# An attention and expert kernel whose order is made by a planner: a shared port in its rules, a shift per kind of task, and two pairs of heads in fp32

## The chip, the cores and the metric

The kernel runs on one core of a Trainium2 chip. The metric is the time of one execution in microseconds on the device; three executions of the kernel before are given by their median and their lowest and highest. The profile shows one further execution. Its engines are TensorE (PE, with its weight loads as PEld), VectorE (DVE), ScalarE (ACT), GpSimd (POOL) and SyncE (SP), which here issues nearly all transfers.

## The reference

Attention over 4 batches, 8 heads, 1152 keys and 64 dimensions, with queries averaged in pairs (576 of them), followed by a two-matrix expert layer with an ELU between:

```python
q_pool = q.reshape(B, H, S // 2, 2, D).mean(axis=3)
scores = np.matmul(q_pool, k.transpose(0, 1, 3, 2)) / np.sqrt(D)
attn = np.exp(scores - scores.max(-1, keepdims=True))
attn = attn / (attn.sum(-1, keepdims=True) + 1e-09)
x = np.matmul(attn, v)                      # (4, 8, 576, 64) -> 2304 tokens x 512
h = x @ w_in                                # 512 x 2048
g = np.where(h > 0, h, np.exp(np.minimum(h, 0)) - 1)
out = g @ w_out                             # 2048 x 512
```

All inputs and the output are fp32 (the weights arrive in a 64-bit form and are decoded on the chip).

## The kernel before

The work of a batch is cut into 4 pairs of heads, and a pair into 9 steps: 8 steps of 128 queries of one head (4 tiles, 2 heads) and one step with the last 64 queries of both heads. There are 144 steps in all. A step's tasks are: the scores on TensorE (L728 to L740), the score pass on VectorE (L746), which scales the scores from PSUM into the SBUF tile `ep` and keeps their extreme, the exponential with its sum on ScalarE (L752), and the reciprocal (L760, L761). Then one of two ways follows, by the table `SPLIT`, a letter for each pair of each batch:

- `s`, split: the probabilities are written as an fp16 high half `hb` (L791 on ScalarE or L788 on GpSimd) and an fp16 low half (L794, VectorE, a scale-and-subtract with two SBUF inputs); both are transposed by SP's DMAs (L800) into `pT`, and the product with the values takes 54 fp16 matmuls (L863). The values are split as well (L453, then L465 on VectorE or L411 with L471 on GpSimd).
- `f`, fp32: the probabilities are normalized in place (L764 GpSimd, L767 VectorE or L770 ScalarE), transposed on TensorE in 9 matmuls (L819), copied from PSUM into `pT` in three copies of 384 columns (L829 ScalarE, or a VectorE copy), and the product with the values is in fp32 (L851).

Keys, queries, expert inputs `x` and weights are always held as two fp16 halves, high and low, scaled by a power of two that a small chain finds (`across`: transpose, largest value, matmul back). The low halves of keys, queries and values run on VectorE (L465) or, as a scaling and a subtraction, on GpSimd (L411, L471). The expert layer of a batch is done in two groups of tokens (256 and 320), as soon as the attention outputs of all four pairs are there: first matrix (L965), ELU (L978, L981, L986, L991), high and low halves of `g` (L1005 or L1013; L1009 or L1017), second matrix (L1036), output.

The order of the work on every engine is not written out; a planner makes it. `Plan.add` records tasks with an engine, a duration, a key and, for some, other engines on which they may run. `Plan.run` then plays the program in time on five engines and at each moment gives a free engine the ready task of the lowest key; a task goes to another engine when that engine's duration plus a penalty is not over the work that stands ahead of it on its own. The order in which tasks start there is the order of the program. The numbers in `CFG` are offsets of the keys, penalties and step lengths. Durations of the class `Port` mark tasks that use the port that VectorE and GpSimd share. Before, two such tasks side by side were played at a reduced speed:

```python
def shares():
    d, p = busy["DVE"], busy["POOL"]
    if d is not None and p is not None and isinstance(d.dur, Port):
        return 0.72 if isinstance(p.dur, Port) else 0.55
    return 1.0
```

Of the kernel before, what the change touches and what calls it, by code (L numbers as in the profile page):

```python
# [19 lines left out]
    LOADS=-40491, WI0=-5900, WIT=9652, WO0=5372132, WOT=32390, T0=500, T1=500, M0=16259,  # L20
    M1=61275, KS=33293, KM=-17450, KE=21505, KH=-783, KL=19371, KV=-12117, KN=-1335, KX=-18428,
    KO=-16558, PEN=-19222, W0L=2523, WIN=5632, PD=20862, KS0=87938, KM0=-10021, KE0=9571,
    KH0=4598, KL0=8793, KV0=-437, KX0=-10633, PLM0=0, NS0=36, PLM=0, M2=5934, DP=0, FK=0,
    PENW=-13761, PENH=-11637, FL=2000, PH0=2, PH=1, KT=18640, KT0=8763, LV=45661, PENN=-27979,
    PENT=17079, PLP=1, WLP=1, HIP=0, PA=-1616, PB=6775, KA=-8245, KB=-28775, KC=3162,
# [3 lines left out]
SPLIT = ("ffff", "ssss", "ssss", "ssss")  # L29


class Port(float):
    pass
# [29 lines left out]
class Plan:  # L63
# [7 lines left out]
    def __init__(self):  # L71
        self.tasks, self.slots, self.make, self.lend = [], {}, {}, {}
# [43 lines left out]
    def run(self):  # L116
# [38 lines left out]
        while done < len(self.tasks):  # L155
# [5 lines left out]
            while again:  # L161
                again = False
                for e in engines:
# [29 lines left out]
                    rest[e] = float(t.dur)  # L193
# [15 lines left out]
            ends = [now + rest[e] / rate[e] for e in engines if busy[e] is not None]  # L209
# [13 lines left out]
            for e in engines:  # L223
# [3 lines left out]
                if rest[e] <= 1e-3:  # L227
                    t = busy[e]
                    busy[e] = None
# [22 lines left out]
def attention_moe_kernel(  # L252
# [165 lines left out]
    def across(src, n, key, after, bufs, take):  # L418
# [3 lines left out]
        def turn():  # L422
            nc.tensor.transpose(xp.ap[0:n, 0:128], src(), ident)

# [7 lines left out]
        t1 = plan.add("PE", 200.0, key, turn, after, [xp] + bufs)  # L432
        t2 = plan.add("DVE", 440.0, key, most, [t1], [xp, xr])
        t3 = plan.add("PE", 310.0, key, back, [t2], [xp, xr])
        return plan.add("DVE", 600.0, key, lambda: take(xp.ap[:, 256:256 + n]), [t3], [xp] + bufs)


    def prep(pr, t0, t1):
# [7 lines left out]
        def absum(dst, src, j):  # L446
            def f():
                nc.scalar.activation(out=dst(), in_=src(), func=AF.Abs, accum_out=sm.ap[:, j:j + 1])
            return f

        def hi(dst, src, j):
            def f():
                nc.scalar.activation(out=dst(), in_=src(), func=AF.Copy, scale=sm.ap[:, 8 + j:9 + j])  # L453

            def g():
                ts(nc.gpsimd, dst(), src(), sm.ap[:, 8 + j:9 + j], 1.0)
            return f, g

        def lo(dst, src, h, j):
            def f():  # L460
# [8 lines left out]
            def g():  # L469
                ts(nc.gpsimd, src(), src(), sm.ap[:, 8 + j:9 + j], 1.0)  # L470
                nc.gpsimd.tensor_tensor(out=dst(), in0=src(), in1=h(), op=ALU.subtract)  # L471
            return f, g

        def halves(n, kh, kl, dst_h, dst_l, src, j, after, bufs):
# [3 lines left out]
            t = plan.add("DVE", dve(n), kl, f, [h], bufs, [("POOL", Port(pol(n) + pol2(n)), g)] if CFG["PLP"] else [])  # L478
# [16 lines left out]
        def load(src, dst):  # L495
            def f():
# [3 lines left out]
            return f  # L500

        def qadd(eng):
            def f():
                qs = q32.ap[:, :nq, 0]
                eng.tensor_tensor(out=qs, in0=qs, in1=q32.ap[:, :nq, 1], op=ALU.add)
            return f
# [12 lines left out]
        sums.append(plan.add("ACT", act(1152) + 90.0, key[1], absum(k_h, k_s, 1), [tk], [kn, k32, sm]))  # L519
        if pr.split:  # L520
            v16 = pr.v16 = plan.buf("v16", "v32")
            v_s, v_h, v_l = (lambda: v32.ap), (lambda: v16.ap[:, :, :, 0]), (lambda: v16.ap[:, :, :, 1])
            sums.append(plan.add("ACT", act(1152) + 90.0, key[2], absum(k_h, v_s, 2), [tv, sums[1]], [kn, v32, sm]))
# [38 lines left out]
    for pr in pairs:  # L562
        if pr.i == 0:
# [4 lines left out]
    first_keys = pairs[0].kl  # L568

# [15 lines left out]
    def weights(which, g, t0, t1):  # L585
# [5 lines left out]
        for s in range(2):  # L591
            def load(s=s, raw=raws[s]):
# [7 lines left out]
            lds.append(plan.add("DMA", Move(490.0, 1700.0), CFG["W0L"] + s if g + which == 0 else t0 - 14000.0 + s, load, (), [raws[s]]))  # L600
# [285 lines left out]
    for st in steps:  # L886
        attention(st)
# [217 lines left out]
```

## Time and profile before

| what | value |
|---|---|
| median of 3 executions | 866.14 us (865.11 to 869.76) |
| the profiled execution | 859.8 us, span 857.9 us |
| granted TensorE clock, mean | 0.977 |
| busy TensorE / VectorE / ScalarE / GpSimd | 734.2 / 705.2 / 605.2 / 407.4 us |
| TensorE waiting for the score pass (L746) | 44.5 us in 45 waits |
| instructions | 19937 |

The profiled execution is some 0.7% shorter than the median of the others. Times of instructions are read from it, so a sum is made against 859.8 us and then put beside 866.1 us. A busy share counts the time in which an engine had an instruction running; that includes the time in which a running instruction stood still.

### The profile page before, as it was taken

The page shows a single profiled execution, that of the slowest core. Times are in us where ns is not written, and L with a number is a line of the kernel's source. Part 1 is how long each engine was busy: PE and PEld are TensorE (multiplying, and loading weights), DVE is VectorE, ACT ScalarE, POOL GpSimd, SP SyncE. Part 2 cuts the span into 40 slices and gives each one's busy share as a digit, 9 for nine tenths or more (in the row PEclk, how much of TensorE's full clock was granted, in tenths as well). Part 3 has the DMA queues.
Part 4 walks back from the last instruction along what each step waited for, and adds up shares of the span by engine and source line. Part 5 has one row for each costly group of instructions (what it writes and reads, how often), then busy time and mean ns, then how long its engine had stood idle before and what let it go on. Part 6 is the DMA issues. An engine that isn't in the chain of part 4 may idle for free. (4 is left out here: it accounts for less than half of the span.)

```text
span 857.9 us, 19937 instructions
## 1 busy us (share of the span) xinstructions
PE 734.2 (86%) x7839; PEld 474.3 (55%) x7839; DVE 705.2 (82%) x1308; ACT 605.2 (71%) x1019; POOL 407.4 (47%) x356
## 2 busy tenths in 40 slices
PE   1268789687978989997989999979998999999997
PEld 0136566466754565555765565547745655576553
DVE  7799898998998899988889698987998898975140
ACT  3478889898886788676788677777866775665250
POOL 1444343436999559313576364223764583035120
PEclk9999999999999999998999999979999999999999
DMA  8955719432959999998998999999889999950000
GB/s 284 264 111 154 194 34 295 157 76 36 218 129 168 179 176 225 177 192 180 183 178 168 200 181 210 191 187 219 170 162 169 216 153 158 185 106 2 25 2 31
DMA packets 353438, 136.06 MB, mean 159 GB/s; under 512 B 315200, under 2 KB 333632, under 8 KB 353344
## 3 DMA queue, kind: packets, MB, share of 16 engines
q1 hardware_dynamic: 353344, 134.79, 78.3%
q8 instruction: 61, 1.00, 0.5%
q14 instruction: 33, 0.27, 0.1%
HBM read 45.09 MB, written 4.72 MB: 58 GB/s over the span
## 5 line engine op out<-in xcount | busy, mean ns | idle before, releaser
L746 DVE TENSOR_SCALAR_CACHE_REDUCE ep<-s,sm 128x1152 f32<-128x1152 f32 x144 | 203.3, 1412 | 28.5 <-PE s L740 13.2
L752 ACT ACTIVATE ep<-ep,wk 128x1152 f32<-128x1152 f32 x144 | 180.4, 1253 | 51.5 <-DVE ep L746 42.7
L965 PE MATMUL r<-x,wi 128*128 128x256 f16 (+1 forms) x1536 | 203.6, 291 | 7.4 <-DVE x L876 2.3
L794 DVE SCALAR_TENSOR_TENSOR ep<-ep,wk,hb 128x1152 f16<-128x1152 f32 x108 | 174.3, 1617 | 14.6 <-POOL hb L788 8.0
L1036 PE MATMUL r<-wo,g 128*128 128x512 f16 (+1 forms) x888 | 179.7, 380 | 1.0 <-ACT x L872 1.0
L965 PEld LDWEIGHTS <-wi 128*128 128x128 f16 x1536 | 149.4, 99 | 53.5 <-issue 10.8
L728 PE MATMUL s<-kT,qT 128*128 128x512 f16 (+2 forms) x480 | 98.5, 338 | 50.0 <-DVE ep L746 44.5
L1036 PEld LDWEIGHTS <-g 128*128 128x128 f16 (+1 forms) x888 | 75.2, 100 | 89.9 <-issue 8.3
L791 ACT ACTIVATE hb<-ep,wk 128x1152 f16<-128x1152 f32 x68 | 85.1, 1252 | 51.6 <-issue 18.3
L788 POOL TENSOR_SCALAR hb<-ep,wk 128x1152 f16<-128x1152 f32 x40 | 56.4, 1410 | 123.8 <-DVE wk L761 66.1
L986 POOL TENSOR_SCALAR tmp<-tmp,us 128x320 f32<-128x320 f32 (+1 forms) x96 | 73.6, 769 | 84.5 <-ACT tmp L981 75.8
L863 PE MATMUL r<-pT,v 128*64 128x128 f16 (+1 forms) x3240 | 97.2, 218 | 3.7 <-DMA pT<-hb 3.2
L863 PEld LDWEIGHTS <-v 128*64 128x64 f16 x3240 | 87.9, 112 | 18.3 <-issue 17.4
L728 PEld LDWEIGHTS <-qT 128*128 128x128 f16 (+1 forms) x480 | 40.4, 101 | 92.6 <-issue 53.6
L991 DVE SCALAR_TENSOR_TENSOR tmp<-r,wk,tmp 128x320 f32<-128x320 f32 (+1 forms) x96 | 57.2, 607 | 32.4 <-POOL tmp L986 32.2
L978 ACT ACTIVATE tmp<-r 128x320 f32<-128x320 f32 (+1 forms) x96 | 45.6, 479 | 21.6 <-PE r L965 14.5
L819 PE MATMUL r<-ident,ep 128*128 128x128 f32 x324 | 48.4, 297 | 13.9 <-ACT ep L770 5.0
L981 ACT ACTIVATE tmp<-tmp,us 128x320 f32<-128x320 f32 (+1 forms) x96 | 58.2, 610 | 1.8
L740 PE MATMUL s<-kT,qT 64*128 64x512 f16 (+1 forms) x320 | 58.6, 404 | 0.0
L1017 DVE TENSOR_TENSOR g<-tmp,g 128x320 f16<-128x320 f32 (+1 forms) x49 | 43.3, 888 | 11.0 <-ACT g L1005 9.1
L819 PEld LDWEIGHTS r<-ident,ep 128*128 128x128 f32 x324 | 37.9, 150 | 23.9 <-issue 8.8
L829 ACT ACTIVATE pT<-r 128x384 f32<-128x384 f32 x108 | 45.9, 491 | 6.3 <-PE r L819 5.2
(125 smaller groups left out, 1017.8 us busy)
## 6 DMA issues: line engine op xcount, KB each, us to landing
k<-in_k_dram SPq DMA_DIRECT2D x16, 576.0 KB, 5.3
v<-in_v_dram SPq DMA_DIRECT2D x16, 576.0 KB, 5.4
q<-in_q_dram SPq DMA_DIRECT2D x32, 256.0 KB, 3.5
g<-in_moe_w_out_dram SPq DMA_DIRECT2D x14, 512.0 KB, 5.8
qT<-qT SPq DMA_DIRECT2D x48, 144.0 KB, 3.1
g<-in_moe_w_in_dram SPq DMA_DIRECT2D x13, 512.0 KB, 4.7
out_dram<-tmp SPq DMA_DIRECT2D x16, 256.0 KB, 2.7
pT<-hb SPq DMA_TRANSPOSE x108, 3.5
```

The lines of the kernel that those rows point to most:

```text
L728: nc.tensor.matmul(s.ap[rows, c, 0:n], pr.qT.ap[:, 0, j, rows], keys[h][c], start=True, stop=False, skip_group_check=True,)
L740: nc.tensor.matmul(s.ap[rows, c, 0:512], pr.qT.ap[r, 1, j, rows], keys[h][c][r], start=False, stop=True, skip_group_check=True,)
L746: nc.vector.tensor_scalar(e_(), s.ap.rearrange("p a b -> p (a b)")[:, 0:S], pr.sm.ap[:, 12:13], None, op0=ALU.mult, op1=ALU.min, accum_out ...
L752: nc.scalar.activation(out=e_(), in_=e_(), func=AF.Exp, bias=nm.ap[:, 0:1], scale=-1.0, accum_out=nm.ap[:, 1:2],)
L791: nc.scalar.activation(out=hb.ap, in_=e_(), func=AF.Copy, scale=nm.ap[:, 1:2])
L794: nc.vector.scalar_tensor_tensor(out=e16(), in0=e_(), scalar=nm.ap[:, 1:2], in1=hb.ap, op0=ALU.mult, op1=ALU.subtract)
L819: nc.tensor.transpose(tp.ap[:, c * 128:(c + 1) * 128], e_()[:, (j + c) * 128:(j + c + 1) * 128], ident)
L863: nc.tensor.matmul(half(h), pr.v16.ap[:, h, order[c], e], p, start=(j + c == 0), stop=(j == 2 and c == NCH - 1), skip_group_check=True,)
L965: nc.tensor.matmul(hp.ap[:, f * n:(f + 1) * n], w_in16[g][:, a, c, (f0 + f) * 128:(f0 + f + 1) * 128], x16.ap[:, e, c, g0:g0 + n], start=( ...
L981: nc.scalar.activation(out=en.ap[:, :m], in_=en.ap[:, :m], func=AF.Exp, scale=us.ap[:, 8 + g:9 + g])
L986: nc.gpsimd.tensor_scalar(en.ap[:, :m], en.ap[:, :m], -1.0, us.ap[:, 5:6], op0=ALU.add, op1=ALU.mult)
L1036: nc.tensor.matmul(op.ap[r0:r0 + tn, :], gt[qd].ap[:, a, fi, o:o + tn], w_out16(f // 2)[:, e, f % 2, :], start=(i < 128 // tn), stop=(i >= ...
```

## The change

The planner's model of the shared port becomes a turn: a VectorE task marked `Port` and any GpSimd task exclude each other, the later one stands still until the earlier one is done, and a task can be given as several parts, each of which takes the port anew. Each task gets a kind (the name of its emitting function and the batch it belongs to), and a new table `NUDGE` shifts the key of each kind in each batch. The numbers of `CFG` and some durations are new. `SPLIT` turns the second and fourth pair of batch 1 from split to fp32.

```diff
+NUDGE = {
+    "absum_act00": 3011, "absum_act01": -1969058, "absum_act02": -15538, "absum_act03": -297,
...
-SPLIT = ("ffff", "ssss", "ssss", "ssss")
+SPLIT = ("ffff", "sfsf", "ssss", "ssss")
...
+        m = super().__new__(cls, sum(parts))
+        m.parts = parts
...
+        t.kind = emit.__name__ + self.at
+        t.key += NUDGE.get(t.kind, 0)
...
-        def shares():
-            d, p = busy["DVE"], busy["POOL"]
-            if d is not None and p is not None and isinstance(d.dur, Port):
-                return 0.72 if isinstance(p.dur, Port) else 0.55
-            return 1.0
+        port, more, stuck = [None], {e: [] for e in engines}, set()
+
+        def enter(e, parts):
+            rest[e], more[e] = float(parts[0]), list(parts[1:])
+            if e != "POOL" and not isinstance(busy[e].dur, Port):
+                return
+            if port[0] is None:
+                port[0] = e
+            else:
+                stuck.add(e)
+
+        def leave(e):
+            if port[0] == e:
+                port[0] = stuck.pop() if stuck else None
...
-            share = shares()
-            rate = {e: share if e in ("DVE", "POOL") else 1.0 for e in engines}
+            rate = {e: 0.0 if e in stuck else 1.0 for e in engines}
...
+                    leave(e)
+                    if more[e]:
+                        enter(e, more[e])
+                        continue
...
-            t = plan.add("DVE", dve(n), kl, f, [h], bufs, [("POOL", Port(pol(n) + pol2(n)), g)] if CFG["PLP"] else [])
+            t = plan.add("DVE", dve(n), kl, f, [h], bufs, [("POOL", Port(pol(n), pol2(n)), g)] if CFG["PLP"] else [])
...
-        sums.append(plan.add("ACT", act(1152) + 90.0, key[1], absum(k_h, k_s, 1), [tk], [kn, k32, sm]))
+        sums.append(plan.add("ACT", act(1152) - 15.0, key[1], absum(k_h, k_s, 1), [tk], [kn, k32, sm]))
...
-            td = plan.add("DVE", Port(2000.0), t0 + s, dec, [lds[s]] + ([first_keys] if CFG["FK"] else []), [raws[s], us[s]] + to)
+            td = plan.add("DVE", Port(615.0, 615.0, 615.0), t0 + s, dec, [lds[s]] + ([first_keys] if CFG["FK"] else []), [raws[s], us[s]] + to)
...
-                tq = plan.add("ACT", 410.0, t0 - K("KL", u) + j, out_act, [tt], [tp, pT], [("DVE", 480.0, out_dve)])
+                tq = plan.add("ACT", 380.0, t0 - K("KL", u) + j, out_act, [tt], [tp, pT], [("DVE", 480.0, out_dve)])
```

Counted over the whole program, VectorE's scale-and-subtract passes go from 108 to 90 on probabilities, from 6 to 32 on halves of keys, from 13 to 16 on queries and from 4 to 10 on values; its copies of 384 columns from PSUM to `pT` go from none to 37, its expert low halves from 51 to 42. GpSimd's scalings and subtractions for keys (13 each), values (8 each) and queries (3 each) all go, and its normalizing passes go from 19 to 34. TensorE's transposes of probabilities go from 324 to 486 and its 54-matmul products from 60 to 50. ScalarE writes 49 high halves `hb` where it wrote 68, and 125 copies to `pT` where it wrote 108. In the program's order 72 matmuls of the first expert matrix now stand ahead of the last score pass of batch 0, where there were none. In both orders all of the first matrix's work of batch 3 stands behind that batch's last scores.

The start shows where the first keys' low half goes. On GpSimd these were the first instructions of the program that worked on keys (`k`, `kn`), queries (`q`) and weights (`h`, `g`, `wi`) before:

```order
L505 TENSOR_TENSOR q_90<-q_90 128x9x64
L411 TENSOR_SCALAR h_78<-h_78,wk 128x512
L667 TENSOR_TENSOR wi_62<-h_78,wi_62 128x512
L411 TENSOR_SCALAR k_103<-k_103,sm_134 128x1152
L471 TENSOR_TENSOR kn_138<-k_103,kn_138 128x9x128
L505 TENSOR_TENSOR q_185<-q_185 128x9x64
```

And on VectorE these rows stand there now, from the low half of the first queries (`qn`) to the first weights behind the keys:

```order
L544 SCALAR_TENSOR_TENSOR qn_145<-q_90,sm_146,qn_145 128x9x64
L721 TENSOR_SCALAR wk<-r_162 128x1
L478 TENSOR_SCALAR wk<-wk 128x1
L479 TENSOR_SCALAR wk<-wk 128x1
L723 TENSOR_SCALAR wk<-wk 128x1
L544 SCALAR_TENSOR_TENSOR kn_148<-k_104,sm_146,kn_148 128x9x64 x2
L745 SCALAR_TENSOR_TENSOR wi_61<-g_86,wk,wi_61 128x512
```

The keys' low half moved from two GpSimd instructions to two VectorE passes, five instructions behind the query's.

SP's queue at the same place, from the transpose of the first queries to the last copy that the first scores need (L547), was before:

```order
L538 DMA_TRANSPOSE qT_181<-qn_133 128x9x128
L485 DMA q_185<-in_q_dram 128x4x128
L490 DMA q_185<-in_q_dram 64x128
L485 DMA q_185<-in_q_dram 128x4x128
L490 DMA q_185<-in_q_dram 64x128
L598 DMA g_195<-in_moe_w_in_dram 128x2x512
L550 DMA_TRANSPOSE kT_203<-kn_138 128x18x128
L544 DMA qT_181<-qT_181 64x1152 x2
L598 DMA g_228<-in_moe_w_in_dram 128x2x512
L497 DMA k_233<-in_k_dram 128x2x576
L547 DMA qT_181<-qT_181 64x1152
```

Now it is, up to the same copy (L629):

```order
L620 DMA_TRANSPOSE qT_190<-qn_145 128x9x128
L632 DMA_TRANSPOSE kT_199<-kn_148 128x18x128
L626 DMA qT_190<-qT_190 64x1152 x2
L682 DMA g_214<-in_moe_w_in_dram 128x2x512
L682 DMA g_216<-in_moe_w_in_dram 128x2x512
L578 DMA k_221<-in_k_dram 128x2x576
L629 DMA qT_190<-qT_190 64x1152
```

The four query loads moved ahead of the first transpose, and the weight load that stood between the two transposes moved behind them.

In batch 1 TensorE's rows change. Before, behind a step's scores (`s`) there stood the expert matmuls on `x` and `wi`, here those that follow the last step of a pair:

```order
L740 LDWEIGHTS qT_2218
L740 MATMUL s_3402<-kT_2330,qT_2218 64x512
L423 MATMUL r_3417<-ident,sm_3180 3x128
L965 LDWEIGHTS wi_63
L965 MATMUL r_3419<-x_2101,wi_63 128x320
```

Now a stretch of the same batch reads as follows, between two steps of the fourth pair (`ep` are probabilities, L906 their transposes, L938 the fp32 product):

```order
L826 MATMUL s_3621<-kT_2995,qT_3077 128x512
L906 MATMUL r_3632<-ident,ep_3527 128x128 x3
L938 MATMUL r_3637<-pT_3541,v_2023 64x128 x18
L906 MATMUL r_3663<-ident,ep_3527 128x128 x3
L814 LDWEIGHTS qT_3077
L814 MATMUL s_3672<-kT_2995,qT_3077 128x512
```

Transposes and fp32 products have come between the scores of the converted pairs, and the expert matmuls moved to other places of the batch.

## Rows read from the trace of the kernel before

**Rows 1.** The page's first part: busy time, share of the span, instructions.
```profile
PE 734.2 (86%) x7839; PEld 474.3 (55%) x7839; DVE 705.2 (82%) x1308; ACT 605.2 (71%) x1019; POOL 407.4 (47%) x356
```

**Rows 2.** Busy time by stretch; columns as in the first line.
```profile
core 0: us, PE busy (x) PEld busy (x) DVE busy (x) ACT busy (x) POOL busy (x), PEclk, DMA share, GB/s
0.00:43.00 43.00, 6.74 (x22) 3.52 (x23) 31.28 (x72) 18.22 (x36) 12.52 (x16) 1.00 0.88 273
43.00:757.00 714.00, 632.27 (x7104) 411.21 (x7103) 639.19 (x1174) 544.88 (x908) 369.72 (x308) 0.97 0.88 170
121.00:201.00 80.00, 62.70 (x654) 46.07 (x654) 73.65 (x156) 69.57 (x148) 34.59 (x26) 0.96 0.52 151
201.00:303.00 102.00, 88.88 (x963) 59.21 (x963) 90.97 (x156) 78.44 (x127) 79.24 (x61) 0.98 0.83 155
303.00:386.00 83.00, 78.99 (x939) 47.04 (x934) 76.32 (x137) 62.56 (x103) 44.70 (x41) 1.00 1.05 190
664.00:855.00 191.00, 184.81 (x1820) 114.16 (x1818) 118.78 (x217) 107.18 (x175) 64.06 (x69) 1.00 0.53 98
757.00:858.00 101.00, 95.19 (x717) 59.62 (x714) 34.70 (x64) 42.06 (x77) 25.16 (x33) 0.99 0.12 27
```

**Rows 3.** TensorE's waits: for whom, us in total, times, longest.
```profile
PE s L728 <- DVE ep L746: 44.5, 45, 4.5
```

**Rows 4.** The start in order of time: start, us, engine, line, operation.
```profile
22.34 0.81 DVE L465 SCALAR_TENSOR_TENSOR qn<-q,sm,qn 128x576 f16<-128x576 f32 x1
23.07 0.15 DVE L637 TENSOR_SCALAR wk<-r 128x1 f32<-128x1 f32 x1
...
24.32 2.36 POOL L471 TENSOR_TENSOR kn<-k,kn 128x1152 f16<-128x1152 f32 x1
24.41 3.48 DVE L661 SCALAR_TENSOR_TENSOR wi<-g,wk,wi 128x512 f16<-128x512 f32 x2 [0.63 <-ACT wi L658]
...
28.28 0.53 SPq L598 DMA_DIRECT2D g<-in_moe_w_in_dram  x1
28.91 3.72 SPq L550 DMA_TRANSPOSE kT<-kn  x1
32.72 1.18 SPq L544 DMA_DIRECT2D qT<-qT  x2
36.69 0.47 SPq L547 DMA_DIRECT2D qT<-qT  x1
40.97 1.12 PE L728 MATMUL s<-kT,qT 128*128 128x512 f16 x3 [3.12 <-DMA qT<-qT]
```

**Rows 5.** VectorE's passes with no GpSimd pass beside them, in order of time.
```profile
740.01 1.41 DVE L794 SCALAR_TENSOR_TENSOR ep<-ep,wk,hb 128x1152 f16<-128x1152 f32 x1
789.45 0.49 DVE L1017 TENSOR_TENSOR g<-tmp,g 128x320 f16<-128x320 f32 x1 [0.54 <-ACT g L1005]
```

**Rows 6.** VectorE's groups by form: count, busy us, mean ns, idle before.
```profile
L794 DVE SCALAR_TENSOR_TENSOR ep<-ep,wk,hb 128x1152 f16<-128x1152 f32 x108 | 174.3, 1617 | 14.6 <-POOL hb L788 8.0 <-ACT hb L791 6.3
L1017 DVE TENSOR_TENSOR g<-tmp,g 128x320 f16<-128x320 f32 x36 | 30.7, 856 | 8.5 <-ACT g L1005 6.9 <-POOL g L1013 1.3
L465 DVE SCALAR_TENSOR_TENSOR qn<-q,sm,qn 128x576 f16<-128x576 f32 x13 | 16.1, 1235 | 0.0
L465 DVE SCALAR_TENSOR_TENSOR kn<-k,sm,kn 128x576 f16<-128x576 f32 x6 | 7.4, 1273 | 0.0
```

**Rows 7.** GpSimd's groups by form: low halves and normalizing.
```profile
L471 POOL TENSOR_TENSOR kn<-k,kn 128x1152 f16<-128x1152 f32 x13 | 34.4, 2647 | 1.1
L764 POOL TENSOR_SCALAR ep<-ep,wk 128x1152 f32<-128x1152 f32 x19 | 23.9, 1259 | 54.6 <-DVE wk L761 19.5 <-DVE x L878 11.2 <-ACT pT L829 8.3
L471 POOL TENSOR_TENSOR v<-v,v 128x1152 f16<-128x1152 f32 x8 | 21.2, 2646 | 0.7
L411 POOL TENSOR_SCALAR k<-k,sm 128x1152 f32<-128x1152 f32 x13 | 18.0, 1385 | 21.6 <-ACT kn L453 21.6
```

**Rows 8.** TensorE in order of time: transposes, fp32 product, split product.
```profile
87.05 2.19 PE L851 MATMUL r<-pT,v 128*64 128x128 f32 x36 [0.59 <-ACT pT L829]
92.84 1.20 PE L819 MATMUL r<-ident,ep 128*128 128x128 f32 x9
731.84 1.70 PE L863 MATMUL r<-pT,v 128*64 128x128 f16 x54
```

**Rows 9.** ScalarE's copy of transposed probabilities, by form.
```profile
L829 ACT ACTIVATE pT<-r 128x384 f32<-128x384 f32 x108 | 45.9, 491 | 6.3 <-PE r L819 5.2
```

More of the change, by code (lines that the diff above doesn't have):

```diff
@@ L19, with __new__ @@
 CFG = dict(
[L20 to L25, printed above, removed]
-)
-SPLIT = ("ffff", "ssss", "ssss", "ssss")
+    LOADS=-2465884, WI0=-27823, WIT=30440, WO0=1311932, WOT=4783, T0=1480, T1=812, M0=21242,
+    M1=58392, KS=5164412, KM=-16195, KE=597808, KH=-20226, KL=126077, KV=-42119, KN=-15967,
+    KX=-43605, KO=-36554, PEN=-18129, W0L=26355, WIN=-42633, PD=3605, KS0=29075649, KM0=3580,
+    KE0=43169, KH0=-7128, KL0=17190, KV0=-37362, KX0=35076, PLM0=0, NS0=36, PLM=0, M2=6438, DP=0,
+    FK=0, PENW=-13844, PENH=10146, FL=2000, PH0=2, PH=1, KT=140078, KT0=-327, LV=15492, PENN=-24464,
+    PENT=-48259, PLP=1, WLP=1, HIP=0, PA=9244, PB=93473, KA=40989, KB=-4257737, KC=34460,
+)
+NUDGE = {
[43 rows of a table added]
+    "turn0": -32562, "w_hii": -11591, "w_hio": 455, "w_loi": 299, "w_loo": -451, "wi_mino": -21137,
[8 rows of a table added]
+}
+SPLIT = ("ffff", "sfsf", "ssss", "ssss")
 class Port(float):
-    pass
+    def __new__(cls, *parts):
+        m = super().__new__(cls, sum(parts))
+        m.parts = parts
+        return m
 class Move(float):
@@ L204, in run @@
                     again = True
-            share = shares()
-            rate = {e: share if e in ("DVE", "POOL") else 1.0 for e in engines}
+            rate = {e: 0.0 if e in stuck else 1.0 for e in engines}
             if cold:
                 rate["PE"] = self.COLD
-            ends = [now + rest[e] / rate[e] for e in engines if busy[e] is not None]
+            ends = [now + rest[e] / rate[e] for e in engines if busy[e] is not None and rate[e]]
             if landing:
@@ L420, in across, with across_turn, across_take @@
         xr, xp = plan.buf("xr"), plan.buf("r")
-        def turn():
+        def across_turn():
             nc.tensor.transpose(xp.ap[0:n, 0:128], src(), ident)
+        def across_take():
+            take(xp.ap[:, 256:256 + n])
         def most():
@@ L430, in back @@
             nc.tensor.matmul(xp.ap[:, 256:256 + n], ones[0:n].to_broadcast([n, 128]), xr.ap[0:n, 1:1 + n], start=True, stop=True)
-        t1 = plan.add("PE", 200.0, key, turn, after, [xp] + bufs)
-        t2 = plan.add("DVE", 440.0, key, most, [t1], [xp, xr])
+        t1 = plan.add("PE", 200.0, key, across_turn, after, [xp] + bufs)
+        t2 = plan.add("DVE", Port(440.0), key, most, [t1], [xp, xr])
         t3 = plan.add("PE", 310.0, key, back, [t2], [xp, xr])
-        return plan.add("DVE", 600.0, key, lambda: take(xp.ap[:, 256:256 + n]), [t3], [xp] + bufs)
+        return plan.add("DVE", Port(600.0), key, across_take, [t3], [xp] + bufs)
     def prep(pr, t0, t1):
@@ L522, in prep @@
             v_s, v_h, v_l = (lambda: v32.ap), (lambda: v16.ap[:, :, :, 0]), (lambda: v16.ap[:, :, :, 1])
-            sums.append(plan.add("ACT", act(1152) + 90.0, key[2], absum(k_h, v_s, 2), [tv, sums[1]], [kn, v32, sm]))
+            sums.append(plan.add("ACT", act(1152) - 15.0, key[2], absum(k_h, v_s, 2), [tv, sums[1]], [kn, v32, sm]))
         def up(top):
@@ L591, in weights, with load_w @@
         for s in range(2):
-            def load(s=s, raw=raws[s]):
+            def load_w(s=s, raw=raws[s]):
                 view = raw_words(raw).rearrange("p (c f) t -> p c f t", c=nch)
@@ L598, in load @@
                 nc.sync.dma_start(out=view, in_=src)
-            lds.append(plan.add("DMA", Move(490.0, 1700.0), CFG["W0L"] + s if g + which == 0 else t0 - 14000.0 + s, load, (), [raws[s]]))
+            lds.append(plan.add("DMA", Move(490.0, 1700.0), CFG["W0L"] + s if g + which == 0 else t0 - 14000.0 + s, load_w, (), [raws[s]]))
         def dst(s):
@@ L663, in lo, with w_lo_pool @@
                 )
-            def lo_pool(x=x, cs=cs):
+            def w_lo_pool(x=x, cs=cs):
                 ts(nc.gpsimd, x(), x(), c, 1.0)
                 nc.gpsimd.tensor_tensor(out=to()[:, 1, cs], in0=x(), in1=to()[:, 0, cs], op=ALU.subtract)
-            h = plan.add("ACT", act(512) + 80.0, t0, hi, after, bf)
-            ends.append(plan.add("DVE", Port(700.0), t0, lo, [h], bf, [("POOL", Port(pol(512) + pol2(512)), lo_pool)] if CFG["WLP"] else []))
+            h = plan.add("ACT", act(512) + 80.0, t0, w_hi, after, bf)
+            ends.append(plan.add("DVE", Port(665.0), t0, w_lo, [h], bf, [("POOL", Port(pol(512), pol2(512)), w_lo_pool)] if CFG["WLP"] else []))
             ends[-1].pen = CFG["PENW"]
@@ L802, in f @@
                     )
-                return f
+                p_turn.__name__ += str(j)
+                return p_turn
             hw = [("ACT", act(S), phi_act), ("POOL", pol(S), phi)]
@@ L933, in experts @@
         txs = across(lambda: us.ap[:, 0:1], 1, t0, [txr], [us], xup)
-        txd = plan.add("DVE", 220.0, t0, xdown, [txs, w_fin], [us])
+        txd = plan.add("DVE", Port(220.0), t0, xdown, [txs, w_fin], [us])
         txd2 = plan.add("DVE", 140.0, t0, xdown2, [txd, wo_fin], [us])
```

46 lines of the change are left out of this document (29 added, 17 removed), and 50 rows, old and new, of the table NUDGE.

## The prediction

> **What bounds the kernel now.** I read the page's busy shares first [rows 1]: TensorE is busy 86% of a span of 857.9 us, VectorE 82%, ScalarE 71%, GpSimd 47%. No engine is full over the whole span, so the next view is the busy time by stretch [rows 2]. The reader is to see three regimes. Until 43 us TensorE does almost nothing (6.7 us): the weights are decoded and the first keys are made ready. From 43 to 757 us VectorE is busy 639 of 714 us (89.5%) and TensorE 632 (88.6%). From 757 us on TensorE alone counts: it is busy 95 of 101 us with the last batch's two expert matrices, and VectorE a third of the time. So the middle has two engines near their limit that wait for each other in turn. The waits say in which direction: the largest single wait of TensorE is for the score pass of VectorE, 44.5 us in 45 waits [rows 3]. That TensorE can run almost without gaps is seen in the stretch from 664 to 855 us, busy 184.8 of 191 [rows 2]; the longest idle shares of TensorE lie where batch 0 ends and batch 1 begins, 17.3 us of the 80 before 201 us and 13.1 of the 102 behind it.
>
> The second thing to see is what VectorE's passes wait for while they run. At 24.41 us two scale-and-subtract passes on weights took 3.48 us together; a GpSimd subtraction on keys had begun at 24.32 and ran 2.36 us, and the two end 1.2 us behind it [rows 4]. One such pass on 576 elements had taken 0.81 us just before [rows 4], and the 1152-element low half of the probabilities takes 1.41 us alone [rows 5] but 1617 ns in the mean of 108 [rows 6]. VectorE's busy time therefore contains waiting. The groups give its size, mean less the time alone, times the count: probabilities (1617 - 1410) x 108 = 22 us, expert low halves (856 - 490) x 36 = 13 us, query halves (1235 - 810) x 13 = 5.5 us, key halves (1273 - 810) x 6 = 2.8 us [rows 4 to 6]. Together 44 us; smaller groups come on top, which I leave out.
>
> The Trainium skill states this as a rule (SBUF — State Buffer, Who interferes with whom): a VectorE pass with two SBUF inputs and a GpSimd instruction that reads SBUF take turns on one port pair, and the later one "**fully blocks**". The rows at 24.4 us agree with it. By the planner's old rule, in which both run on at 0.72 of their speed, the pair of passes would have lost 0.28 of 2.27 us of overlap, 0.6 us; by turns it loses all of it, and 3.48 us less two passes of some 0.7 us is 2.1. Were the old rule right, the 30 us taken below for the waiting would be 8 and the sum 24 us higher, 875.
>
> **The change part by part.** *The planner's rule and the shifts* add no instruction; they move them. Three moves carry weight.
>
> First, the low halves of keys, values and queries leave GpSimd entirely. GpSimd loses 13 key pairs of (1385 + 2647) ns = 52 us and 8 value subtractions of 2646 ns with a scaling pass that I price as the keys', 32 us; it gains 15 normalizing passes of 1259 ns, 19 us [rows 7]. That is about 65 of its 407 us. VectorE gets 26 more half-key passes and 3 more query passes of 0.81 us and 6 value passes of 1.41 us: 21 + 2.4 + 8.5 = 32 us [rows 4, 5].
>
> Second, at the start the first keys' low half now stands on VectorE behind the query's. The query pass began at 22.34 us and took 0.81; four passes of 0.15 us follow, then two key halves, so the keys are ready at about 23.15 + 0.65 + 1.6 = 25.4 us. In the trace GpSimd ended them at 26.7, and the transpose was issued only at 28.91 us behind a weight load [rows 4]; in the new SP order no load stands between. Everything to the first scores hangs on SP in order: transpose issue 3.72 us, copies at 32.72 and 36.69, first scores at 40.97 [rows 4]. I take 3.4 us earlier, rounded to 4 with what follows quicker; the bounds are nothing (a weight load that now stands ahead of the last query copy waits instead) and 6.
>
> Third, 72 matmuls on the first expert matrix stand ahead of batch 0's last score pass, where none stood. They go into TensorE's idle time before 201 us and cost nothing there; without that cover they would cost what they cost now.
>
> *Two split pairs of batch 1 turn fp32.* Removed on VectorE: 18 probability low halves of 1.41 us = 25 us; the new split of work also takes 9 expert low halves off it, 4.5 us at 0.49 [rows 5]. Added: 37 PSUM copies of 384 columns. VectorE has no such copy in the trace; ScalarE's takes 491 ns [rows 9], the bounds are 0.2 and 0.8 us, and I take ScalarE's: 18 us. ScalarE itself loses 19 high halves and gains 17 copies, and stays clear of its limit. The 36 fewer DMA transposes free SP and a buffer, and are priced at nothing.
>
> TensorE pays. A step's nine fp32 transposes take 1.20 us and there are 18 steps more: 21.6 us. The value product takes 2.19 us in fp32 and 1.70 us split, 8 times: 4 us [rows 8]. Together 26 us. The steps lie between 121 and 386 us, where TensorE has 17.3 + 13.1 + 4.0 = 34 us idle [rows 2], and their own VectorE work is lighter by a pass of 1.41 us each, which is the pass that TensorE waits behind. I take all 26 as covered; without cover it costs all 26.
>
> *VectorE's sum.* Alone it changes by 32 + 18 - 25 - 4.5 = about +20 us. Against that stands the waiting of 44 us. The least that goes is GpSimd's share, 65/407 = 16% of it, 7 us; the most is all 44. I take 30, because what leaves GpSimd are its longest pieces, up to 2.65 us, and what is left is half as long, and because the new planner does not place the two against each other where it has a choice. VectorE thus gains 10 us, at the share of 0.895 at which it is busy in the middle 11 us.
>
> *The sum.* The profiled execution took 859.8 us (span 857.9). 859.8 - 4 (start) - 11 (VectorE) + 0 (TensorE, covered) = 845. The median of the runs, 866.1, lies 6.3 us above that execution; the forecast is given in the same terms, 845 + 6 = **851 us**. The tail of 101 us stays: all 24 first-matrix groups of the last batch stand behind its last score in both orders.
>
> **The rivals.**
> *TensorE becomes the bound (slower).* The place is batch 1, 201 to 386 us, where a converted step puts three transpose groups and a longer product on TensorE between two scores. For it: TensorE is busy 88.6% of the middle already, and its 82 idle us there come in small pieces behind VectorE, which a longer queue need not fill. Against it: the stretch with 97%. If half of the 26 us is uncovered and VectorE's gain is lost with it, 860 - 4 + 13 + 0 = 869, in the median 875; with all of it 888. It decides from about 20 us uncovered, or 9 when VectorE's gain does not come.
> The skill speaks against this rival (Perfetto Trace Analysis, Identifying the Most-Contended Engine): matmul busy time is a poor measure of how near TensorE is to its limit, and the share of weight loads a better one. That share is 411 of 714 us here, 58% [rows 2]; by that rule TensorE has room and 851 stands.
> *The planner's gain and TensorE's cost cancel (no change).* The waiting falls by 20 instead of 30, just what VectorE takes on, and 4 of the 26 us show: 860 - 4 + 4 = 860, in the median 866.
> *The turns stop costing altogether (much faster).* All 44 us go: VectorE -24, at 0.895 -27, so 860 - 4 - 27 = 829, 835 in the median. TensorE's floor lies just below: 39 us to the first scores, then 734.2 - 6.7 + 26 = 753 us at the share of the best stretch, 0.967: 818, or 826 in the median. What speaks against it: both engines would have to be as dense all along as TensorE alone is at the end.
>
> **How the numbers follow.** Forecast (835 to 862 us) 0.50; much faster (under 835) 0.12; no change 0.14; TensorE the bound 0.24. A measurement here tells 0.5% from nothing, so faster means under 861.8 and slower above 870.5: faster 0.62, same 0.14, slower 0.24. The range leaves out the lowest part of the third rival, below 825, and the TensorE case with most of its cost uncovered, above 879: 825 to 879. The likeliest case's own range is 835 to 862.
>
> **What the profile would show.** First scores near 37 us instead of 41. GpSimd busy near 340 us, no key or value group on it. The mean of the probability pass near 1.45 us instead of 1617 ns, and the expert low half near 0.55. VectorE busy about 695 us. TensorE busy near 760 us with its idle time between 121 and 386 us nearly gone; the score pass no longer its main releaser. The forecast is wrong if TensorE's idle time in the middle stays near 82 us, or if the probability pass stays above 1.55 us.

## The result, and the profile after

| what | before | after |
|---|---|---|
| median of the runs, same chip | 865.62 us | 841.68 us (838.87 to 844.75) |
| ratio | | 0.9722 [0.9667, 0.9777] |
| a second comparison | 864.25 us | 840.74 us, 0.9745 [0.9715, 0.9775] |
| profiled execution (span) | 859.8 (857.9) us | 844.75 (843.0) us |

The forecast was 851.0 us with a range of 825 to 879, a gain of 15 us; the medians give 24. The profiled execution of before is one of its shortest and that of after its longest, so the two traces differ by 15 us where the medians differ by 24; that these 15 equal the forecast's is chance. A second profile of the changed kernel (836.4 us, span 834.6) is used where the difference matters.

The page's first part of the changed kernel answers to [rows 1]: TensorE is busier by 16 us, VectorE less by 23, GpSimd by 78.

```profile
PE 750.6 (89%) x7821; PEld 493.3 (59%) x7821; DVE 682.2 (81%) x1352; ACT 594.3 (71%) x1024; POOL 329.3 (39%) x318
```

TensorE's wait for the score pass, in the view of waits, answers to [rows 3]: 28 waits where there were 45, and still its largest.

```profile
PE s L814 <- DVE ep L832: 28.3, 28, 2.5
```

To see where the time went, both traces are cut at the same points of the work: the ends of the 18th, the 72nd and the 144th (last) score pass, which are half of batch 0, the end of batch 1, and the end of batch 3. The kernel before, busy time by stretch (columns as in [rows 2]):

```profile
0.00:121.00 121.00, 67.80 (x585) 46.46 (x586) 103.39 (x226) 83.75 (x163) 45.38 (x40) 0.99 0.65 183
121.00:386.10 265.10, 230.65 (x2545) 152.31 (x2545) 241.05 (x448) 210.68 (x375) 158.63 (x127) 0.98 0.81 165
386.10:756.80 370.70, 340.35 (x3993) 215.78 (x3993) 325.83 (x575) 268.48 (x405) 178.24 (x158) 0.97 1.01 182
756.80:858.00 101.20, 95.39 (x719) 59.80 (x716) 34.90 (x65) 42.26 (x77) 25.16 (x33) 0.99 0.11 27
```

The changed kernel, the same view at the same points:

```profile
0.00:116.60 116.60, 67.09 (x583) 46.61 (x584) 98.06 (x227) 78.46 (x149) 34.41 (x34) 0.99 0.67 188
116.60:382.10 265.50, 247.99 (x2556) 170.17 (x2557) 235.50 (x483) 211.84 (x390) 117.14 (x105) 0.98 0.63 136
382.10:738.20 356.10, 336.60 (x3908) 213.64 (x3906) 311.27 (x577) 262.03 (x411) 152.54 (x147) 0.99 0.99 180
738.20:843.00 104.80, 98.91 (x785) 62.89 (x779) 37.34 (x69) 41.98 (x77) 25.23 (x34) 0.99 0.13 29
```

Line by line: the first stretch is 4.4 us shorter, and VectorE is busy 5.3 less in it. The second, which holds the converted pairs, is as long as before (+0.4): VectorE is busy 5.6 less there, TensorE 17.3 more. The third, in which no pair was converted (only the last two steps of batch 1 reach into it), is 14.6 us shorter, and VectorE is busy 14.6 less. The tail is 3.6 longer, with 3.5 us more of TensorE work in it: 785 matmuls for 719, where the third has 3908 for 3993. Some of the third's gain is thus work that moved into the tail, and the two together are 11 us shorter. The second profile of the changed kernel has the stretches at 113.8, 261.4, 354.6 and 104.8 us, so a single stretch is uncertain by some 4 us. The third with its tail stays the largest part, 11 of 15 us in the first profile and 12 of 23 in the second.

VectorE's groups by form in the changed kernel (count, busy us, mean ns, idle before) answer to [rows 6]:

```profile
L880 DVE SCALAR_TENSOR_TENSOR ep<-ep,wk,hb 128x1152 f16<-128x1152 f32 x90 | 136.0, 1518 | 6.8 <-POOL hb L874 5.1 <-ACT hb L877 1.4
L544 DVE SCALAR_TENSOR_TENSOR kn<-k,sm,kn 128x576 f16<-128x576 f32 x32 | 27.7, 905 | 0.7 <-ACT kn L530 0.7
L1105 DVE TENSOR_TENSOR g<-tmp,g 128x320 f16<-128x320 f32 x33 | 22.9, 700 | 8.2 <-ACT g L1093 6.3 <-POOL g L1101 1.5
L919 DVE COPY pT<-r 128x384 f32<-128x384 f32 x37 | 19.5, 551 | 2.4 <-PE r L906 2.3
L544 DVE SCALAR_TENSOR_TENSOR qn<-q,sm,qn 128x576 f16<-128x576 f32 x16 | 13.9, 871 | 0.7 <-ACT qn L530 0.6
```

Every mean that has a counterpart fell, those of the halves of keys and queries to within 0.1 us of the time alone (0.81).

### The profile page after: what moved, and what is told of

Its sections match the earlier page's. It is cut to its first block, busy times and chain, and to the rows that moved or that the text cites. A ratio compares the mean times of both kernels' runs of the same rounds, so it can differ in the third digit from the quotient of the medians.

```text
span 843.0 us, 19849 instructions
## 1 busy us (share of the span) xinstructions
PE 750.6 (89%) x7821; PEld 493.3 (59%) x7821; DVE 682.2 (81%) x1352; ACT 594.3 (71%) x1024; POOL 329.3 (39%) x318
## 5 line engine op out<-in xcount | busy, mean ns | idle before, releaser
L880 DVE SCALAR_TENSOR_TENSOR ep<-ep,wk,hb 128x1152 f16<-128x1152 f32 x90 | 136.0, 1518 | 6.8 <-POOL hb L874 5.1
L850 POOL TENSOR_SCALAR ep<-ep,wk 128x1152 f32<-128x1152 f32 x34 | 42.4, 1247 | 114.7 <-DVE wk L847 30.6
L877 ACT ACTIVATE hb<-ep,wk 128x1152 f16<-128x1152 f32 x49 | 61.4, 1252 | 32.0 <-issue 8.2
L950 PE MATMUL r<-pT,v 128*64 128x128 f16 (+1 forms) x2700 | 79.0, 215 | 2.9 <-DVE tmp L1079 1.0
L950 PEld LDWEIGHTS <-v 128*64 128x64 f16 x2700 | 71.9, 110 | 14.2 <-issue 12.5
L906 PE MATMUL r<-ident,ep 128*128 128x128 f32 x486 | 70.5, 292 | 3.2 <-ACT ep L856 2.4
L1097 POOL TENSOR_TENSOR g<-tmp,g 128x320 f16<-128x320 f32 (+1 forms) x49 | 55.8, 1143 | 25.1 <-ACT g L1093 24.1
L906 PEld LDWEIGHTS r<-ident,ep 128*128 128x128 f32 x486 | 55.1, 147 | 17.3 <-issue 9.9
L938 PE MATMUL r<-pT,v 128*64 128x128 f32 (+1 forms) x1080 | 61.0, 268 | 1.8 <-ACT pT L916 1.7
L916 ACT ACTIVATE pT<-r 128x384 f32<-128x384 f32 x125 | 53.7, 489 | 10.7 <-PE r L906 9.5
```

What stands on the lines that cost most here:

```text
L877: nc.scalar.activation(out=hb.ap, in_=e_(), func=AF.Copy, scale=nm.ap[:, 1:2])
L880: nc.vector.scalar_tensor_tensor(out=e16(), in0=e_(), scalar=nm.ap[:, 1:2], in1=hb.ap, op0=ALU.mult, op1=ALU.subtract)
L906: nc.tensor.transpose(tp.ap[:, c * 128:(c + 1) * 128], e_()[:, (j + c) * 128:(j + c + 1) * 128], ident)
L938: nc.tensor.matmul(half(h), pr.v32.ap[:, h, order[c]], p, start=(c == 0), stop=(c == NCH - 1), skip_group_check=True,)
L950: nc.tensor.matmul(half(h), pr.v16.ap[:, h, order[c], e], p, start=(j + c == 0), stop=(j == 2 and c == NCH - 1), skip_group_check=True,)
```

## The experiments

The theory at the start: VectorE sets the pace in the middle, part of its busy time is standing still in turns with GpSimd, and TensorE's added work is covered. The rivals: VectorE's added load eats the relief, TensorE becomes the bound, or the planner's order does it all. Times are medians, ratios against the kernel before on the same chip.

**The low halves alone on VectorE** (the kernel before, its order kept; the 24 low halves of keys, queries and values that GpSimd computed are issued on VectorE in the same places):

```diff
+                    if getattr(t, "low", False):
+                        t.emit = t.ways["DVE"][1]
```

> The kernel before with its order kept, but the 24 low halves of keys, values and queries that stood on GpSimd are issued on VectorE at the same places. VectorE gets 26 half-key passes and 3 query passes of 0.81 us and 8 value passes of 1.41 us, 35 us alone; GpSimd loses about 92 us. Theory of turns (what VectorE paid was waiting behind long GpSimd passes): the mean of the probability pass falls from 1617 to under 1540 ns, VectorE's busy time rises by less than 20 us, and the time is 0 to 12 us shorter. Rival (VectorE's own load sets the pace): 35 us at the busy share of 0.895 are added, 20 to 39 us longer.

Measured: 857.24 us against 864.31, 0.9922 [0.9894, 0.995]. VectorE got more work and was busy less, 694.9 us. Its groups by form in this kernel show why:

```profile
L796 DVE SCALAR_TENSOR_TENSOR ep<-ep,wk,hb 128x1152 f16<-128x1152 f32 x108 | 164.2, 1523 | 15.6 <-POOL hb L790 7.8 <-ACT hb L793 7.6
L1019 DVE TENSOR_TENSOR g<-tmp,g 128x320 f16<-128x320 f32 x36 | 21.6, 604 | 8.3 <-ACT g L1007 6.8 <-POOL g L1015 1.3
```

The probability pass is at 1523 ns, where the whole change brings it (1518), from 1617 [rows 6]. So this one move is enough for the whole fall of that mean. Alone it is worth 7 us, where the whole change is worth 24. The Trainium skill's rule of the exclusive port (SBUF — State Buffer, Who interferes with whom) agrees: passes that nobody edited became shorter when GpSimd's long instructions went.

**The low halves back on GpSimd** (the changed kernel, all 42 of them; the same edit with "POOL"):

> The kernel after with its order kept, but all 42 low halves of keys, values and queries are issued on GpSimd as a scaling and a subtraction. VectorE loses 32 x 0.81 + 10 x 1.41 + 16 x 0.81 = 53 us alone, GpSimd gets about 147 us on top of 329. Theory of turns: the mean of the probability pass rises from 1518 to over 1600 ns, VectorE's busy time falls by far less than 53 us, and the time is 10 to 35 us longer than after. Rival (VectorE's load sets the pace, and GpSimd at 39% has room): 0 to 30 us shorter than after.

Measured: 898.8 us, 1.0404 [1.0364, 1.0445], 57 us above the changed kernel. VectorE is busy 651.6 us, 31 less, and the kernel is still much longer; the theory had the direction, and its 10 to 35 us were too few. The probability pass went as it said, from 1518 ns to over 1600:

```profile
L882 DVE SCALAR_TENSOR_TENSOR ep<-ep,wk,hb 128x1152 f16<-128x1152 f32 x90 | 146.3, 1632 | 9.9 <-POOL hb L876 8.5 <-ACT hb L879 1.0
```

Busy time over the whole span, with the granted clock of this run 0.964, shows that TensorE needs more time for the same matmuls:

```profile
sum 899.00, PE 770.99 PEld 502.84 DVE 651.56 ACT 595.68 POOL 456.79; mean PE 192.75 PEld 125.71 DVE 162.89 ACT 148.92 POOL 114.20
```

20 us of the 57 are TensorE's longer busy time (771.0 against 750.6); the rest is waiting, spread over all stretches but the tail. A low half of keys on GpSimd is two instructions of about 2.5 and 1.3 us where VectorE needs two passes of 0.8, so the data come later too; how much of the 57 us that is, and how much the turns, is not shown.

**The transposes of the converted pairs twice** (the changed kernel, +21.6 us of TensorE):

```diff
-                    for c in range(3):
+                    for c in list(range(3)) * (2 if u.i == 1 else 1):
```

> The kernel after with its order kept, and every transpose of the two converted pairs of batch 1 issued twice: 18 steps of 1.2 us more on TensorE, 21.6 us. Theory (what the conversion put on TensorE is covered by its idle time): 0 to 8 us longer than after. Rival (TensorE became the bound with the conversion): 17 to 22 us longer.

Measured: 855.83 us, 0.9907 [0.9875, 0.9938], 14 us above the changed kernel; both sides had expected otherwise. The stretch of the converted pairs takes it:

```profile
114.60:392.40 277.80, 260.40 (x2692) 185.70 (x2692) 236.06 (x482) 212.77 (x389) 115.72 (x105) 0.98 0.59 130
```

It is 12.3 us longer than in the changed kernel with 12.4 us more TensorE time. The 162 transposes did not take the 21.6 us as reckoned: their line went from 70.5 to 86.2 us, 15.7 more. So of a microsecond as reckoned two thirds shows, and of one by which TensorE is really busy longer nearly all. After the change TensorE's time in batch 1 is far from free. The Trainium skill (Perfetto Trace Analysis, Identifying the Most-Contended Engine) would judge TensorE's room by the share of weight loads, 59% of the span here (and by the useful work, not taken here). By that share the added transposes would have found room; here the measurement says otherwise.

**The products of the same two pairs twice in the kernel before** (+15 us of TensorE):

```diff
-            for j, (a, e) in enumerate(((0, 0), (0, 1), (1, 0))):
+            for j, (a, e) in list(enumerate(((0, 0), (0, 1), (1, 0)))) * (2 if u.i == 1 and pr.p % 2 else 1):
```

> The kernel before with its order kept, and the 54-matmul products of the second and fourth pair of batch 1 issued twice: 8 of 1.63 us and 2 of 1.0 us, 15 us more on TensorE. Theory (before the change TensorE's time in batch 1 had cover, so the conversion's TensorE time went where it cost nothing): 0 to 4 us longer than before. Rival (it was already paid for in full there): 11 to 15 us longer.

Measured: 865.7 us against 863.8, 1.003 [1.0004, 1.0055], or 2.6 us (0.3 to 4.8). Before the change a microsecond of TensorE in batch 1 cost 0.17 (0.02 to 0.32). The two prices are of different work: products, which come last in a step, before, and transposes, for which the copies and the product wait, after. No run doubled the same work in both kernels, so how much of the rise from 0.17 to two thirds is owed to the change is not shown.

**The score pass of 18 steps twice** (+25 us of VectorE), in the kernel before and in the changed one (there with the condition `u.i == 1 and not pr.split`, which picks the same 18 steps):

```diff
+            for _ in range(2 if u.i == 1 and pr.p % 2 else 1):
                 nc.vector.tensor_scalar(
```

> The kernel before with its order kept, and the score pass of the 18 steps of the second and fourth pair of batch 1 issued twice: 25 us more on VectorE. Theory (VectorE set the pace there, so that the conversion's 25 us off VectorE were worth most of their length): 15 to 28 us longer than before. Rival (VectorE's time there is covered by what it waits for): 0 to 8 us longer. Together with the doubled products this prices the conversion: 25 us of VectorE at one price against 26 us of TensorE at the other.

> The kernel after with its order kept, and the score pass of the 18 steps of the two converted pairs issued twice: 25 us more on VectorE, at the same steps whose low-half passes the conversion took away. Theory (VectorE is the engine that sets the pace in batch 1, so that taking 25 us off it was worth something): 10 to 28 us longer than after. Rival (batch 1 goes at TensorE's pace now): 0 to 6 us longer.

Measured: 884.78 us in the kernel before, 1.0236 [1.0166, 1.0306], 21 us more; 861.9 in the changed one, 0.9977 [0.9957, 0.9998], 20 more. A microsecond of VectorE in batch 1 costs 0.8 before and after. TensorE's wait for the score pass rises with it, here in the changed kernel with the pass twice:

```profile
PE s L814 <- DVE ep L833: 38.8, 39, 2.6
```

**The shifts left out** (the changed kernel, planned anew):

```diff
-        t.key += NUDGE.get(t.kind, 0)
+        t.key += 0
```

> The kernel after, planned anew with the table of shifts left empty; rule, CFG and SPLIT are the new ones. Theory (the order that the shifts make is a large part of the gain): 10 us or more longer than after, with more idle time on TensorE between 43 and 740 us. Rival (the rule of turns and the conversion carry the gain, the shifts are small change): within 5 us of after.

Measured: 872.87 us, 1.0102 [1.0072, 1.0132]: 1% longer than before. TensorE is idle for 66.7 us between 43 and 740 us, where it is 48.4 with the shifts, as the theory had it. So the new rule, the moved low halves, the converted pairs and the new `CFG` gain nothing without the shifts. These numbers of `CFG` belong to the shifts, though; what others would give without shifts was not tried, so the 31 us are the price of taking the shifts away and not their share of the 24. The third stretch of this kernel is where most of it goes:

```profile
393.90:771.70 377.80, 354.14 (x4060) 223.93 (x4057) 326.46 (x602) 265.98 (x406) 148.44 (x142) 0.99 0.92 172
```

It is 21.7 us longer than with the shifts, and VectorE is busy 15.2 us more there, as much as before the change. TensorE is busy 17.5 us longer, in part with work that stands in the neighbouring stretches when the shifts are there (4060 matmuls for 3908).

**The old sharing rule in the planner** (the changed kernel with the new tables):

```diff
-            rate = {e: 0.0 if e in stuck else 1.0 for e in engines}
+            share = (0.72 if isinstance(busy["POOL"].dur, Port) else 0.55) if both else 1.0
+            rate = {e: share if e in ("DVE", "POOL") else 1.0 for e in engines}
```

> The kernel after, planned anew with the old rule of the shared port (both run on at 0.72 or 0.55); shifts, CFG, durations and SPLIT are the new ones. Theory (the rule decides where VectorE and GpSimd are set against each other): 8 us or more longer than after, the mean of the probability pass over 1560 ns. Rival (shifts and CFG fix the order, whatever the rule): within 5 us of after, the mean near 1518 ns.

Measured: 882.2 us, 1.0203 [1.0162, 1.0244]. The time is where the theory put it, but not for its reason: the probability pass does not stand longer.

```profile
L882 DVE SCALAR_TENSOR_TENSOR ep<-ep,wk,hb 128x1152 f16<-128x1152 f32 x90 | 136.0, 1512 | 11.3 <-ACT hb L879 9.9 <-POOL hb L876 1.3
```

1512 ns, as in the changed kernel. The first 18 score passes end at 134.7 us, 18 later than in the changed kernel, and the first scores begin at 47.39. That the shifts do not fit this order, as they belong to the other rule, is the likely reason and not shown. The rule's own worth is thereby not measured. Without shifts the planner finds no order with the old rule, and none for the kernel before with the new rule or with the new pairs; nor does it find one for the changed kernel with the old pairs. So no run separates the rule or the conversion from the rest.

**The start.** Two kernels move entries of SP's queue in the changed kernel. The first puts the last query copy right behind the two copies before it; the second also puts the second pair's query loads, with their pair sum, behind that copy:

```diff
+        order.insert(kinds.index("q_lo0") + 1, order.pop(kinds.index("q_hi0")))
...
+        late = [order.pop(i) for i in reversed(early)]
+        order[at:at] = late[::-1]
```

> The changed kernel itself, once more, beside the two with another start so that these can be put against it on the same chip. Expected: 840 to 844 us, 0.972 of the kernel before. No theory hangs on it but this: if it falls outside 838 to 846, differences of 3 us between kernels timed in different calls mean nothing.

> The changed kernel with one instruction of SP's queue moved: the first pair's last query copy stands right behind the two copies before it, ahead of two weight loads and a load of keys; nothing else moves. Both theories expect that it is issued at much the same time (it waits for the two copies before it to land, at 34.7 us in the changed kernel) but lands some 4 us later, as before the change, and not 7.5, so that the first scores begin near 39 us where they began at 42.3. Theory (the start is on the path that sets the end, and the forecast's start step failed by SP's order alone): 2 to 4 us less than the changed kernel, 837 to 840. Rival (the weights decoded on VectorE and the later queries set the pace of the first batch, so that an earlier first score only waits later): within 1 us of it, 841 to 843, and the eighteenth score pass ends at much the same time as in the changed kernel, 116.6 us.

> As the kernel with the earlier last query copy, and the second pair's four query loads and its pair sum stand behind that copy instead of ahead of the first transpose, where SP stood until 24.1 us for their buffer. Both theories expect the first transpose near 24 us, the keys' near 26.2, the copies near 29.2 and 33, the first scores near 37 us, which is what the forecast said. The second pair's queries come some 8 us later. Theory (the start is on the path): 4 to 6 us less than the changed kernel, 835 to 838. Rival (an earlier first score waits later): 841 to 843, with the eighteenth score pass within 1 us of 116.6; above 844 if the late queries of the second pair hold up the third and later steps.

Measured: 840.74 us for the changed kernel itself, 840.49 for the first, 845.22 for the second. TensorE and VectorE of the first in order of time:

```profile
38.06 0.57 DVE L699 TENSOR_SCALAR tmp<-g 128x512 uint32<-128x512 uint32 x1 [4.29 <-DMA g<-in_moe_w_in_dram]
39.99 0.15 DVE L720 TENSOR_REDUCE wk<-wk 128x1 f32<-128x2 f32 x1
40.20 0.37 PE L499 MATMUL r<-ident,wk 128*1 128x128 f32 x1 [7.19 <-DVE wk L720]
40.37 1.16 PE L817 MATMUL s<-kT,qT 128*128 128x512 f16 x3
```

The first scores now wait for no copy. They stand on TensorE behind the transpose of the weights' maximum, which waits for VectorE, which waits 4.29 us for weights that were loaded later. In the second kernel it is the same transpose, later:

```profile
42.58 0.37 PE L504 MATMUL r<-ident,wk 128*1 128x128 f32 x1 [10.52 <-DVE wk L725]
42.74 1.17 PE L822 MATMUL s<-kT,qT 128*128 128x512 f16 x3
```

So the rival was right on the first kernel. In neither did the first scores come when both sides expected them (39 and 37 us, against 40.37 and 42.74). The second kernel is 4.5 us longer than the changed one. Its eighteenth score pass ends at 117.1 us, where the two profiles of the changed kernel have 116.6 and 113.8, with first scores at 42.27 and 40.90. It delays the first scores and the second pair's queries at once; which of them costs the 4.5 us is not shown. What speeds up the queries at the weights' expense gained nothing.

## Why the prediction came out as it did, point by point

**The bound.** That VectorE set the pace before is shown for batch 1: 25 us more of it cost 21, and 15 us more of TensorE cost 2.6. The forecast took 1.12 us of time for a microsecond of VectorE (1/0.895); the runs give 0.8.

**The start (-4 by earlier first scores) failed.** SP's queue in the changed kernel:

```profile
24.12 0.37 SPq L566 DMA_DIRECT2D q<-in_q_dram  x1
...
26.28 1.86 SPq L620 DMA_TRANSPOSE qT<-qn  x1
28.26 2.87 SPq L632 DMA_TRANSPOSE kT<-kn  x1
31.23 1.18 SPq L626 DMA_DIRECT2D qT<-qT  x2
32.50 1.07 SPq L682 DMA_DIRECT2D g<-in_moe_w_in_dram  x2
33.62 0.49 SPq L578 DMA_DIRECT2D k<-in_k_dram  x1
34.71 0.47 SPq L629 DMA_DIRECT2D qT<-qT  x1
```

And TensorE:

```profile
40.32 0.37 PE L496 MATMUL r<-ident,wk 128*1 128x128 f32 x1 [6.48 <-DVE wk L717]
42.27 1.14 PE L814 MATMUL s<-kT,qT 128*128 128x512 f16 x3 [1.58 <-DMA qT<-qT]
```

The first scores came at 42.27 us (40.90 in the second profile), where I had 37 and the kernel before 40.97. I had said "in the new SP order no load stands between", and overlooked what stands in three places. Four query loads now stand ahead of the first transpose, so the keys' transpose came at 28.26 us where it had been 28.91 [rows 4]. Two weight loads and a load of keys stand ahead of the last copy, whose data the scores awaited until 42.27, 7.6 us after its issue, where it had been 4.3 [rows 4]. And on TensorE the weights' maximum stands ahead of the scores, so that nothing before 40.7 was possible. The first stretch still ended 4.4 us earlier, with 5.3 us less VectorE time in it. That the term's size came out was luck.

**VectorE (-10 net) was mis-sized.** It went from 705.2 to 682.2, -23 us. The groups that I priced came out close in sum: key, query and value halves +26, copies +19.5 (forecast 18; 551 ns for 491), probabilities -38, expert halves -16, together about -9; weight halves, which I did not price, +2 (12 passes for 8). By the forecast's own formula 21 of the 44 us of waiting are left: (1518 - 1410) x 90 + (700 - 490) x 33 + (871 - 810) x 16 + (905 - 810) x 32 ns. So 23 went where I took 30, and the expert halves stayed at 700 ns where I had said 0.55 us. The missing 16 us lie in the "smaller groups" that I left out, a few of which only lost passes to other engines. The largest fall, from 12.1 to 7.2 us, is in the scales' passes of one to three columns (L406, now L479). The most for a single pass is in one of 8 columns, here before and then after:

```profile
L920 DVE TENSOR_SCALAR us<-wk,us 128x8 f32<-128x8 f32 x8 | 5.8, 719 | 0.0
```

```profile
L1008 DVE TENSOR_SCALAR us<-wk,us 128x8 f32<-128x8 f32 x8 | 2.1, 257 | 0.1
```

Of my two reasons for the relief, the first (the longest pieces leave GpSimd) is shown by the low halves moved alone. The second (the planner does not place the two against each other) is not: with the old rule the probability pass stands no longer.

**TensorE (+26, covered)** held in time and not in its picture. The stretch of batch 1 did not grow (265.5 us for 265.1), and the first matrix's 72 matmuls did find room in the second half of batch 0 (TensorE idle 11.1 us where it was 17.3, in a stretch of 81.1 us for 80). But TensorE's idle time in the whole stretch went from 34.4 to 17.5 us, not to nearly nothing, and no more than 5.6 us came off VectorE. By the measured prices, 0.8 for VectorE and 0.17 to 0.65 for TensorE, the conversion alone is an estimate of -5 (18 passes of 1.41 us less 19.5 us of copies, times 0.8) and +4 to +17 (26 us as reckoned): no gain, perhaps a loss. By the forecast's terms it was -8 (25 less 18 us of VectorE, divided by 0.895), with TensorE free.

**What I did not price: the order.** 14.6 of the 15 us by which the traces differ (11 with the tail) lie in batches 2 and 3, where no pair was converted. What the low halves alone do there cannot be read from this row of their kernel, as its execution is 4.6 us above its median and that of before 4.5 below:

```profile
384.70:758.90 374.20, 343.19 (x3993) 216.86 (x3990) 321.58 (x593) 267.38 (x405) 139.40 (x135) 0.96 0.99 180
```

Without the shifts it has 377.8 us, with them 356.1. There the shifts bring 15.2 us less VectorE time, a third of it because expert halves went to GpSimd (on VectorE 22.4 us in 20 passes before, 12.8 in 17 without the shifts, 7.1 in 10 with them, summed over the groups of the stretch). The lower clock, as below, took 24 us of this stretch before, 10 without the shifts and 7 with them. Which shifts do it, and how much is owed to what, stays open.

**The rivals.** The time of the rival in which TensorE becomes the bound (875 and more in the median) did not come, but part of its mechanism may be there: further TensorE time in batch 1 now costs two thirds as reckoned, not far below VectorE's 0.8. Nothing cancelled. The time lies between the forecast and the rival in which the turns stop costing (835), but that is not what happened: 21 of 44 us are still there. (That rival's floor of 818 us is 824 in the median, not 826; nothing rests on it.)

**The sum.** That the time came within 10 us of the forecast is in part luck. The start's 4 us came by another way, VectorE lost twice what I had said at a lower price (23 us at 0.8 are 18), the conversion gained nothing that the runs show, and the order was not in the sum. Of the signs that I had named, TensorE's idle time in the middle (48 us, not 82) and the probability pass (1518 ns) fell as they should; the score pass stayed TensorE's main releaser, which I had denied.

## What to carry to other kernels

Price a move between VectorE and GpSimd also by what it takes off the other passes, each by its mean less its time alone, times its count, the small ones too: here 24 low halves moved onto the engine that set the pace made it less busy. Before a step at the start is credited, list what stands ahead of it in every queue that it passes, and what those entries wait for. When a change re-plans the whole order, cut both traces at equal points of the work first, and count the matmuls of each stretch: here the largest part of the gain lay in the two batches in which no pair was converted.

## What the runs showed that was not expected

TensorE's clock fell where it had waited, and the same work then took nearly twice as long. In the kernel before TensorE stood 3.28 us for a score pass at 570 us; the clock granted from 569 to 579 was 0.50, the lower of the two levels, 1.2 GHz. TensorE in order of time, the same product before and in that stretch:

```profile
560.57 1.67 PE L863 MATMUL r<-pT,v 128*64 128x128 f16 x54
...
570.46 1.17 PE L728 MATMUL s<-kT,qT 128*64 128x512 f16 x6 [3.28 <-DVE ep L746]
...
574.84 3.04 PE L863 MATMUL r<-pT,v 128*64 128x128 f16 x53 [2.30 <-DMA pT<-hb]
```

The stretch itself in the view by stretch, with 1.00 in the changed kernel at the same time of its run, where other matmuls stand:

```profile
569.00:579.00 10.00, 6.25 (x72) 4.04 (x72) 9.47 (x20) 6.47 (x10) 5.26 (x3) 0.50 1.04 194
```

```profile
569.00:579.00 10.00, 9.28 (x153) 6.92 (x152) 9.74 (x16) 7.66 (x13) 8.54 (x9) 1.00 1.08 192
```

Summed from the trace, such stretches within the work come to 38 us before and 20 after (mean clock 0.977 and 0.987), and TensorE was busy for 32 and 19 us of them. Half of the 12.5 us between these, some 6, is an estimate of what the clock gave back, and more than half of what is missing between the 26 us that TensorE was to be busier and the 16 that it was. Here a wait cost its own length and then slower matmuls. Not every wait did: one of 2.65 us at 89 us in the kernel before was followed by a clock of 1.00.
